# Batch 0 of a Nyström attention and MLP kernel: two blocks of the second layer beside the first layer's chunks, and a bank for the heads' products

## The chip, the core and the metric

The kernel runs on one core of one Trainium2 chip. The metric is the device time of one execution in microseconds, lower is better. Before the change the median of three runs is 324.2 us (323.54 to 325.01). Five engines work side by side, each in its own program order: TensorE (PE) multiplies, VectorE (DVE) and ScalarE (ACT) do elementwise work and here alone read PSUM, GpSimd (POOL) does elementwise work between SBUF tiles, SyncE (SP) issues DMAs.

## What is computed

For 8 batches with 8 heads of 576 x 64: landmarks are means over 18 rows of q and k (32 each), three softmax matrices are formed, one is inverted by six iterations, and the product gives 576 x 512 rows per batch. A two-layer MLP with a layer norm and a residual follows.

```python
A, Bm, C = sm(q, k_lm), sm(q_lm, k_lm), sm(q_lm, k)
Z = Bm.T / (norm1(Bm) * norminf(Bm) + 1e-6)
for _ in range(6):
    Z = 2 * Z - Z @ Bm @ Z
x = merge_heads(A @ Z @ C @ v)
out = x + relu(layer_norm(x) * g_ln @ w_ch1) @ w_ch2
```

## The kernel before

**The MLP works from the attention's factors.** The first layer's input rows are A times a small matrix per head, so w1 is multiplied by the heads' small matrices first (`product_of_heads`, tile psm, evicted to m), and a chunk m of 128 hidden units is m times ea, the softmax A, with the heads' four products in one 128-row contraction: four matmuls of 288 columns into psh, evicted with a relu into hT (`first_layer`, L758). There are 16 chunks (MCH) per batch, four for each of the four psm. The mean of the layer norm is taken out of w1 once (`less_mean`, psf, L747; `center_w1`, L753) and its scale is applied at the end. The second layer (`second_layer`, L798) takes blocks of 128 rows: 16 matmuls hT times w2 into one PSUM bank (pso), then one DVE instruction that scales and adds the residual rows x (xblk), then a store from SP. There are 36 blocks over all batches, 4 for an even batch and 5 for an odd one; in an even batch the last 64 rows of hT are copied by POOL to the front of the next batch's hT (L802). In batch 0 alone a block is done in two halves of 256 columns, since w2 is loaded and cast in pieces of half the columns (`load_w2`, L210; `cast_w2`, L216).

**Attention.** `attention0` (L282) handles batch 0, `attention2` (L608) the others in sets of batches: (1), (2), (3, 4), (5, 6), (7). In order: psb (landmark scores), psec (scores of k, evicted by ACT's exp to ec and turned by DVE to ecT), psse (norms), pscv (C times v), six times psn with a DVE update st (`iterate`, L425), meanwhile psea (scores of q, exp to ea), and `normalize` (L270), which sums heads by PE (psd), takes Ln and Exp on ACT (lns) and multiplies ea by DVE (batches 0 and 1) or POOL; then pszt and pszc, copied to zt and zcbd. From zt on the first layer of that batch can begin (`ready`). `rows_of` (L439) makes the rows x for the residual and the statistics (psy, xblk, six).

**Preparation.** `Coming` (L459) brings a set: loads (SP), casts to nat (POOL), turns to xT (DVE), and sums over the segments to part, by DVE (`add_up`, two reductions) or by POOL (four additions to asum and s, then a small DVE turn sT), then `spread` (PE psl, ACT lm). `sums_by_dve` says for how many units q is summed by DVE; k always is.

**PSUM.** The pools hold eight banks: ps1 one, ps2 two buffers of two banks (tag p2: pst, psc, psa, psd, psec, psea, psm, psh, pscv, pszt, pszc), psM three buffers of one bank (tag pm: idle, psf, psl, psy, pso, psg and batch 0's small tiles). A buffer is given to the next tile when the last one has been read.

**Order.** Every engine instruction that is wrapped by `keep` stands in the order of the program text, engine by engine. The MLP is a generator, `mlp` (L828), that is advanced by `fill(n)` (L852) by n times 512 columns of PE work wherever the attention leaves room; `mlp` puts one step of the next batch's first layer behind each 2048 columns of the second layer, once that batch is ready, and does the rest alone afterwards. The lists `steps` (L943) say, for each step of an attention, how many columns to fill and how many casts and jobs of the next set to do. Batch 0's prologue is written out by hand (L883 to L939): six iterations with `scale_w1`, `less_mean`, `center_w1` and `warm` matmuls between them, and then fills, jobs of set 1 and rows of batch 0. Helpers record most instructions, so the profile has L75 for matmuls and L69 for DVE, ACT and POOL; the tiles tell them apart.

Of the kernel before, what the change touches and what calls it, by code (L numbers as in the profile page):

```python
# [16 lines left out]
P = 128  # L17
# [3 lines left out]
def kernel(  # L21
# [188 lines left out]
    def load_w2(i):  # L210
        part, m = divmod(i, 4)
        stg = stage.tile([P, 4, DM // 2], FP32, name="wstg", tag="stg")
        keep(nc.sync.dma_start(out=stg[:], in_=w2_src[:, ts(m, 4), ts(part, DM // 2)]))
        w2_coming.append(stg)

    def cast_w2(i):  # L216
        part, m = divmod(i, 4)
        pool.tensor_copy(out=w2_16[:, ts(m, 4), ts(part, DM // 2)], in_=w2_coming[i][:])
# [12 lines left out]
    psM = ctx.enter_context(tc.tile_pool(name="psM", bufs=3, space=bass.MemoryType.PSUM))  # L231

    def warm(n, cols):
        idle = psM.tile([P, 512], FP32, name="idle", tag="pm")
        for _ in range(n):
            MM(idle[:, 0:cols], zeros[:, 0:P], zeros[:, 0:cols])
# [33 lines left out]
    def normalize(ea, engine):  # L270
        pss = ps2.tile([P, 2, 512], FP32, name="psd", tag="p2")
        for half in range(2):
# [4 lines left out]
        engine.tensor_tensor(out=ea, in0=ea, in1=lns[:].rearrange("p a t -> p (a t)"),  # L277
                             op=ALU.mult)
# [3 lines left out]
    def attention0():  # L282
# [58 lines left out]
        def scores_of_q(w):  # L341
            psa = p2([P, NJ, 64], FP32, "psa")
            for (j0, j1) in ((0, 8), (8, NJ)):
                for h in range(4):
# [8 lines left out]
        extra = [lambda: scores_of_q(0), lambda: scores_of_q(1), lambda: product(0),  # L353
                 lambda: product(1), lambda: normalize(ea[0], dve), lambda: normalize(ea[1], dve)]
# [3 lines left out]
        rcv = asm.tile([P, W], FP32, name="rcv", tag="rcv")  # L358
        for it in range(6):
            st = iterate(p1, st, it, W)  # L360
            if it == 4:
# [5 lines left out]
            extra[it]()  # L367
# [16 lines left out]
        ready.add(0)  # L384
        yield "zt"
        for w in range(W):
            dve.tensor_tensor(
                out=zcbd_buf[w][:], in0=pszc[:, w, None, :].broadcast_to([P, 4, D]),
                in1=mask4[:, :, None].broadcast_to([P, 4, D]), op=ALU.mult)
# [49 lines left out]
    def rows_of(bs, ea, zcbd):  # L439
        for i, b in enumerate(bs):  # L440
            t0 = 0
            while t0 < S:
# [4 lines left out]
                psy = psM.tile([P, 512], FP32, name="psy", tag="pm")  # L447
# [11 lines left out]
    class Coming:  # L459
        def __init__(self, bs, sums_by_dve=0):  # L460
            self.bs, self.sums_by_dve = bs, sums_by_dve
# [7 lines left out]
            for i, (nm, w) in enumerate(self.parts[:2 * n]):  # L469
                self.jobs.append((self.turn, i))  # L470
                if nm == "k" or w < sums_by_dve:
                    self.jobs.append((self.add_up, i))
# [25 lines left out]
        def cast(self, i):  # L498
# [11 lines left out]
            if nm == "q" and w >= self.sums_by_dve:  # L510
# [40 lines left out]
        def spread(self, y):  # L551
            part = self.part.pop(y)
            psl = psM.tile([P, 2, 8, LM], FP32, name="psl", tag="pm")
# [54 lines left out]
    def attention2(bs, c):  # L608
# [8 lines left out]
        for y in range(W // 2):  # L617
# [11 lines left out]
            yield  # L629
# [35 lines left out]
        if not late:  # L665
            for y in range(W // 2):
                product(y)
                if y + 1 < W // 2:
                    yield
            product_done()  # L670
        yield

        for it in range(6):
# [9 lines left out]
            yield  # L683
# [10 lines left out]
        for i, b in enumerate(bs):  # L694
            heads[b] = (ea[U * i:U * i + U], zt, U * i)
            ready.add(b)
# [13 lines left out]
        yield  # L710

        yield from rows_of(bs, ea, zcbd_buf[z0:z0 + W])
# [34 lines left out]
    def less_mean(f):  # L747
        psf = psM.tile([P, 512], FP32, name="psf", tag="pm")
        for c in range(KCH):
            MM(psf[:], lesser[:], w1_16[:, c, ts(f, 512)], start=(c == 0), stop=(c == KCH - 1))  # L750
        scalar.copy(less(f), psf[:])

    def center_w1(f, c, n):  # L753
# [4 lines left out]
    def first_layer(b):  # L758
        room_for(b)
        hT, base = hTs[b], 64 * (b % 2)  # L760
        ea, zt, w0 = heads.pop(b)
        m16 = {}

        def product_of_heads(f):
            psm = ps2.tile([P, 2, 512], FP32, name="psm", tag="p2")
            for r in range(2):
                for e in range(2):
                    for u in range(U):
                        block = 2 * r + e if b == 0 else 2 * (e ^ u) + r
                        rows = ds(64 * e, 64)  # L770
                        MM(psm[ds(32 * block, 32), u, :], zt[rows, r, w0 + u, :],
                           w1_16[rows, 2 * u + r, ts(f, 512)], rb=64 * e, cb=32 * block)
            m16[f] = t = mprod.tile([P, U, 512], FP16, name="m16", tag="m16")
            if f % 2 == 0:
                scalar.copy(t[:], psm[:])
            else:
                dve.tensor_copy(out=t[:], in_=psm[:])

        product_of_heads(0)
        yield 512  # L780
        for m in range(MCH):
            f = m // 4
            if b == 0 and m in (1, 4):
                less_mean(2 if m == 1 else 3)
                yield 2048
                center_w1(2 if m == 1 else 3, 0, 4)
            if m % 4 == 1 and f < 3:
                product_of_heads(f + 1)
                yield 512
            psh = ps2.tile([P, 2, 512], FP32, name="psh", tag="p2")  # L790
            for half in range(2):
                for u in range(U):
                    MM(psh[:, half, 0:HS], m16[f][:, u, ts(m % 4, P)], ea[u][:, ts(half, HS)],
                       start=(u == 0), stop=(u == U - 1))
            act(hT[:, m, ds(base, S)].rearrange("p (a t) -> p a t", a=2), psh[:, :, 0:HS], AF.Relu)
            yield 4 * HS

    def second_layer(b):  # L798
        hT = hTs.pop(b)
        if b % 2 == 0:  # L800
            room_for(b + 1)
            pool.tensor_copy(out=hTs[b + 1][:, :, 0:64], in_=hT[:, :, S - 64:S])  # L802
        blocks = range(4 + b % 2)
        order = [(u, None) for u in blocks] if b else [(u, p) for p in (0, 1) for u in blocks]
        for u, p in order:
# [182 lines left out]
```

## Time and profile before

| what | value |
|---|---|
| median of 3 runs | 324.2 us |
| profiled execution, its own time | 323.97 us |
| its span | 321.9 us |
| granted PE clock, mean | 0.968 |
| first chunk of batch 0 (psh) starts | 27.9 us |
| psb of batch 1 starts | 49.2 us |
| first pso starts | 52.2 us |
| psl of batch 2 starts | 83.6 us |
| last chunk's eviction starts | 300.9 us |
| eviction of psh with relu (ACT), mean | 651 ns x128 |
| eviction of psm, ACT and DVE, mean | 1012 and 1207 ns, x16 each |

A line of the timeline gives start, length, engine, source line, operation, output tile<-input tiles, shape and count; in brackets the idle time before it and what ended it. A wait is put down to what came last. PE's busy time is modelled for pipelined matmuls, so the count of columns says more about PE than its busy share.

### The profile page before, as it was taken

To read this page: it belongs to the slowest core of one execution; us is meant where nothing else is said; L and a number is where in the kernel's file an instruction comes from. 1 tells how busy PE (TensorE), PEld (TensorE's weight loads), DVE (VectorE), ACT (ScalarE), POOL (GpSimd) and SP (SyncE) were. 2 spreads that over 40 slices of the span, in tenths; PEclk is the share of its full clock that TensorE was granted. 3 is DMA by queue.
4 is the path that set the end of the run, shared out by engine and by line. 5 is a ranking of instruction groups with operands and counts; after the bars stand their busy time and mean duration, and the time that the engine had idled before them with its cause. 6 is when DMAs were issued, how large, how long until landed. Compare 5 with 4: busy or idle time off the path is not lost.

```text
span 321.9 us, 8232 instructions
## 1 busy us (share of the span) xinstructions
PE 281.5 (87%) x3475; PEld 156.5 (49%) x3475; DVE 172.9 (54%) x369; ACT 175.8 (55%) x289; POOL 127.2 (40%) x154
## 2 busy tenths in 40 slices
PE   7767767989679688999898899999997999999995
PEld 7532434747353344454544444555553455455544
DVE  2555983549776695337995874446450345312112
ACT  2474764437453385595557557675756455454300
POOL 4389975921408996654956413310001100100000
PEclk9996996999799799999999999999999999999999
DMA  7999996164856962850795072111111112121133
GB/s 259 393 386 363 319 264 243 35 179 112 266 164 225 244 210 66 314 170 17 201 279 169 9 186 54 38 35 33 38 40 25 35 35 66 33 59 41 35 82 81
DMA packets 26173, 46.67 MB, mean 145 GB/s; under 512 B 2452, under 2 KB 7832, under 8 KB 26136
## 3 DMA queue, kind: packets, MB, share of 16 engines
q1 hardware_dynamic: 25976, 46.02, 47.6%
q8 instruction: 27, 0.44, 0.6%
q10 hardware_dynamic: 160, 0.13, 0.2%
q14 instruction: 10, 0.08, 0.1%
HBM read 36.70 MB, written 9.44 MB: 143 GB/s over the span
## 4 chain that ended last, share of the span: by engine, by line
PE 58%; DVE 18%; ACT 15%; issue 4%; POOL 2%; DMA 2%; SPq 1%; ACTq 0%; POOLq 0%; DVEq 0%
PE pso L75 29%; PE psh L75 14%; ACT hT L69 5%; DVE six L69 4%; DVE part L69 4%; DVE xT L69 3%; ACT m L69 3%; PE psm L75 3%; DMA stg<-in_k_dram 2%; DVE w L69 2%; PE pscv L75 2%; ACT lns L69 2%; ACT ec L69 2%; PE psec L75 1%; PE psn L75 1%
## 5 line engine op out<-in xcount | busy, mean ns | idle before, releaser
L75 PE MATMUL pso<-w,hT 128*128 128x512 f16 (+1 forms) x656 | 156.0, 360 | 0.0
L69 ACT ACTIVATE hT<-psh 128x576 f16<-128x576 f32 x128 | 81.8, 651 | 56.1 <-PE psh L75 55.4
L75 PE MATMUL psh<-ea,m 128*128 128x288 f16 x512 | 84.5, 290 | 13.8 <-ACT hT L69 5.6
L75 PEld LDWEIGHTS <-hT 128*128 128x128 f16 x656 | 61.3, 100 | 45.8 <-issue 10.2
L75 PEld LDWEIGHTS <-m 128*128 128x128 f16 x512 | 49.9, 99 | 48.2 <-issue 17.8
L69 DVE SCALAR_TENSOR_TENSOR xblk<-pso,rstd,xblk 128x512 f32<-128x512 f32 (+1 forms) x41 | 27.8, 678 | 40.0 <-PE pso L75 39.7
L69 POOL CAST nat<-stg 128x1152 f16<-128x1152 f32 x28 | 32.3, 1169 | 22.5 <-DMA stg<-in_k_dram 9.5
L69 POOL TENSOR_TENSOR ea<-ea,lns 128x576 f16<-128x576 f16 x12 | 15.4, 1284 | 56.7 <-ACT lns L69 56.7
L69 DVE BATCH_NORM_STATS2 six<-xblk 128x6 f32<-128x512 f32 x36 | 24.7, 685 | 20.0 <-ACT xblk L69 19.8
L69 POOL CAST natv<-stg 128x1152 f16<-128x1152 f32 x16 | 18.3, 1164 | 30.2 <-DMA stg<-in_v_dram 27.9
L69 DVE SCALAR_TENSOR_TENSOR st<-st,psn 128x128 f16<-128x128 f16 (+2 forms) x36 | 11.3, 315 | 32.2 <-PE psn L75 32.2
L69 ACT CAST m<-psm 128x1024 f16<-128x1024 f32 x16 | 16.2, 1012 | 20.0 <-PE psm L75 20.0
L69 ACT COPY xblk<-psy 128x512 f32<-128x512 f32 (+1 forms) x40 | 23.4, 588 | 5.2 <-PE psy L75 4.9
L69 DVE CAST m<-psm 128x1024 f16<-128x1024 f32 x16 | 19.3, 1207 | 11.7 <-PE psm L75 11.7
L69 DVE TENSOR_REDUCE part<-xT 128x32 f16<-128x576 f16 x32 | 22.4, 741 | 0.1
L69 DVE STREAM_TRANSPOSE xT<-nat 128x576 uint32<-128x576 uint32 x28 | 21.3, 761 | 1.6 <-POOL nat L69 1.6
L75 PE MATMUL psm<-w,zt 64*32 64x512 f16 x256 | 14.6, 400 | 5.6 <-DVE zt L69 3.8
L69 POOL COPY hT<-hT 128x1024 f16<-128x1024 f16 x4 | 4.1, 1037 | 34.2 <-ACT hT L69 34.2
L75 PE MATMUL psy<-zcbd,ea 128*128 128x256 f16 (+1 forms) x80 | 15.5, 278 | 0.0
L69 POOL TENSOR_TENSOR asum<-nat 128x512 f32<-128x512 f16 x12 | 15.1, 1258 | 1.0
L69 POOL TENSOR_TENSOR asum<-asum 128x256 f32<-128x256 f32 (+1 forms) x24 | 14.2, 592 | 1.9
L69 ACT ACTIVATE ec<-psec 128x576 f16<-128x576 f32 x14 | 10.3, 807 | 3.9 <-PE psec L75 3.9
(108 smaller groups left out, 251.7 us busy)
## 6 DMA issues: line engine op xcount, KB each, us to landing
stg<-in_q_dram SPq DMA_DIRECT2D x16, 576.0 KB, 5.8
stg<-in_k_dram SPq DMA_DIRECT2D x16, 576.0 KB, 6.8
wstg<-in_moe_w_ch_dram SPq DMA_DIRECT2D x16, 512.0 KB, 6.7
out_dram<-xblk SPq DMA_DIRECT2D x62, 128.0 KB, 2.3
stg<-in_v_dram SPq DMA_DIRECT2D x9, 576.0 KB, 6.9
stg<-in_v_dram SPq DMA_DIRECT2D x14, 288.0 KB, 5.1
out_dram<-xblk SPq DMA_DIRECT2D x18, 64.0 KB, 2.0
out_dram<-xblk ACTq DMA_DIRECT2D x2, 64.0 KB, 2.2
```

The costliest lines, as they stand in the source:

```text
L69: return lambda *args, **kw: keep(getattr(self.engine, op)(*args, **kw))
L75: keep(nc.tensor.matmul(o, l, r, start=start, stop=stop, tile_position=(rb, cb), skip_group_check=(skip or cb != 0)))
```

## The change

The second layer's blocks 0 and 1 of batch 0 now accumulate in psM's two buffers while the first layer's chunks are made (`blocks_0_and_1`), behind chunks 9 to 15; `second_layer(0)` keeps blocks 2 and 3, of full width. w2 is loaded and cast in pieces of two whole rows of 128. A new pool psA of one bank takes idle, psf, psm, psl, psy and psg; psm is made for one unit u at a time, half as wide, u 0 evicted by ACT and u 1 by DVE. The prologue is re-ordered: psd in iterations 2 and 3, ea of unit 0 scaled by halves in 3 and 4, that of unit 1 after zt, `less_mean(0)` split, the centering of f 0 after zt, fewer warm calls. DVE evicts chunks 5, 8, 11 and 14 of batch 0, and each third chunk where a first layer runs alone. Attention of batch 1 begins behind chunk 14. A step of the first layer says itself how many columns of the second layer have to follow (`gap`), and none is done while an attention step is `quiet`. `Coming` is given the list of parts that DVE sums. In the code left out psl, psy and psg move to psA, `Coming` looks parts up in that list, and the yields of `attention2` after its scores give True, all others False.

```diff
@@ -208,14 +208,12 @@
-    part, m = divmod(i, 4)
-    stg = stage.tile([P, 4, DM // 2], FP32, name="wstg", tag="stg")
-    keep(nc.sync.dma_start(out=stg[:], in_=w2_src[:, ts(m, 4), ts(part, DM // 2)]))
+    stg = stage.tile([P, 2, DM], FP32, name="wstg", tag="stg")
+    keep(nc.sync.dma_start(out=stg[:], in_=w2_src[:, ts(i, 2), :]))
...
-    part, m = divmod(i, 4)
-    pool.tensor_copy(out=w2_16[:, ts(m, 4), ts(part, DM // 2)], in_=w2_coming[i][:])
+    pool.tensor_copy(out=w2_16[:, ts(i, 2), :], in_=w2_coming[i][:])
@@ -228,10 +226,11 @@
-psM = ctx.enter_context(tc.tile_pool(name="psM", bufs=3, space=bass.MemoryType.PSUM))
+psM = ctx.enter_context(tc.tile_pool(name="psM", bufs=2, space=bass.MemoryType.PSUM))
+psA = ctx.enter_context(tc.tile_pool(name="psA", bufs=1, space=bass.MemoryType.PSUM))
...
-    idle = psM.tile([P, 512], FP32, name="idle", tag="pm")
+    idle = psA.tile([P, 512], FP32, name="idle", tag="pa")
@@ -267,15 +266,17 @@
-def normalize(ea, engine):
+def divisors(ea):
...
-    engine.tensor_tensor(out=ea, in0=ea, in1=lns[:].rearrange("p a t -> p (a t)"),
-                         op=ALU.mult)
+    return lns[:].rearrange("p a t -> p (a t)")
...
+def normalize(ea, engine):
+    engine.tensor_tensor(out=ea, in0=ea, in1=divisors(ea), op=ALU.mult)
@@ -350,21 +351,32 @@
-    extra = [lambda: scores_of_q(0), lambda: scores_of_q(1), lambda: product(0),
-             lambda: product(1), lambda: normalize(ea[0], dve), lambda: normalize(ea[1], dve)]
...
+    lns = []
...
+    def scale_ea(w, half):
+        cols = ts(half, HS)
+        dve.tensor_tensor(out=ea[w][:, cols], in0=ea[w][:, cols], in1=lns[w][:, cols],
+                          op=ALU.mult)
...
     for it in range(6):
         st = iterate(p1, st, it, W)
+        if it < 2:
+            scores_of_q(it)
+        if it in (2, 3):
+            product(it - 2)
+            lns.append(divisors(ea[it - 2]))
...
-        extra[it]()
+        if it in (3, 4):
+            scale_ea(0, it - 3)
         yield "iteration"
@@ -381,8 +393,10 @@
-    ready.add(0)
...
+    scale_ea(1, 0)
+    scale_ea(1, 1)
+    yield "softmax"
@@ -666,9 +680,9 @@
-                yield
+                yield False
...
-    yield
+    yield False
@@ -680,7 +694,7 @@
-        yield
+        yield it < W // 2
@@ -707,9 +720,10 @@
-    yield
...
-    yield from rows_of(bs, ea, zcbd_buf[z0:z0 + W])
+    yield False
+    ready.update(bs)
+    for _ in rows_of(bs, ea, zcbd_buf[z0:z0 + W]):
+        yield False
@@ -744,68 +758,97 @@
-def center_w1(f, c, n):
+psf_of = {}
...
+def less_mean(f, c0=0, c1=KCH):
+    if c0 == 0:
+        psf_of[f] = psA.tile([P, 512], FP32, name="psf", tag="pa")
+    for c in range(c0, c1):
+        MM(psf_of[f][:], lesser[:], w1_16[:, c, ts(f, 512)], start=(c == 0),
+           stop=(c == KCH - 1))
+    if c1 == KCH:
+        scalar.copy(less(f), psf_of.pop(f)[:])
...
+def center_w1(f, c=0, n=KCH):
...
+class First:
+    def __init__(self, b):
+        room_for(b)
+        self.b, self.hT = b, hTs[b]
+        self.ea, self.zt, self.w0 = heads.pop(b)
+        self.m16 = {}
...
+    def product_of_heads(self, f, u):
+        b, zt = self.b, self.zt
+        if u == 0:
+            self.m16[f] = mprod.tile([P, U, 512], FP16, name="m16", tag="m16")
+        psm = psA.tile([P, 512], FP32, name="psm", tag="pa")
         for r in range(2):
             for e in range(2):
...
+                block = 2 * r + e if b == 0 else 2 * (e ^ u) + r
+                rows = ds(64 * e, 64)
+                MM(psm[ds(32 * block, 32), :], zt[rows, r, self.w0 + u, :],
+                   w1_16[rows, 2 * u + r, ts(f, 512)], rb=64 * e, cb=32 * block)
+        t = self.m16[f][:, u, :]
+        if u == 0:
+            scalar.copy(t, psm[:])
         else:
...
+            dve.tensor_copy(out=t, in_=psm[:])
...
+    def chunk(self, m, by_dve=False):
         psh = ps2.tile([P, 2, 512], FP32, name="psh", tag="p2")
         for half in range(2):
             for u in range(U):
...
+                MM(psh[:, half, 0:HS], self.m16[m // 4][:, u, ts(m % 4, P)],
+                   self.ea[u][:, ts(half, HS)], start=(u == 0), stop=(u == U - 1))
+        o = self.hT[:, m, ds(64 * (self.b % 2), S)].rearrange("p (a t) -> p a t", a=2)
+        if by_dve:
+            dve.tensor_scalar(out=o, in0=psh[:, :, 0:HS], scalar1=0.0, scalar2=None,
+                              op0=ALU.max)
+        else:
+            act(o, psh[:, :, 0:HS], AF.Relu)
...
+alone = [False]
...
+def first_layer(b):
+    l1 = First(b)
+    for u in range(U):
+        l1.product_of_heads(0, u)
+        yield 512, 1024
+    for m in range(MCH):
+        f = m // 4
+        if f < 3 and m % 4 in (1, 2):
+            l1.product_of_heads(f + 1, m % 4 - 1)
+            yield 512, 512
+        l1.chunk(m, alone[0] and m % 3 == 2)
+        yield 4 * HS, 2048
...
+def keep_tail(b):
     if b % 2 == 0:
         room_for(b + 1)
...
+        pool.tensor_copy(out=hTs[b + 1][:, :, 0:64], in_=hTs[b][:, :, S - 64:S])
...
+def finish_block(b, u, pso, part=None):
+    j = 9 * (b // 2) + 4 * (b % 2) + u
+    last = j == NBLK - 1
+    cols = ts(part or 0, DM if part is None else DM // 2)
+    x = x_blk[j]
+    dve.scalar_tensor_tensor(out=x[:, cols], in0=pso[:],
+                             scalar=rstds[b][:, u:u + 1], in1=x[:, cols],
+                             op0=ALU.mult, op1=ALU.add)
+    store(j, x, cols, last)
+    if part != 0:
+        x_blk.pop(j)
...
+def second_layer(b):
+    hT = hTs[b]
+    blocks = range(4 + b % 2) if b else (2, 3)
+    for u in blocks:
+        last = b == B - 1 and u == 4
+        for part in ((0, 1) if last else (None,)):
             n = DM if part is None else DM // 2
             cols = ts(part or 0, n)
             pso = psM.tile([P, n], FP32, name="pso", tag="pm")
@@ -816,27 +859,26 @@
+            if u == blocks[-1]:
+                hTs.pop(b, None)
+            finish_block(b, u, pso, part)
...
+quiet = [False]
...
-    yield from first_layer(0)
     for b in range(B):
-        ahead, done, owed = None, False, 0
+        ahead, done, owed, gap = None, False, 0, 0
+        if b:
+            keep_tail(b)
         for cols in second_layer(b):
             yield cols
             if ahead is None and b + 1 in ready:
                 ahead = first_layer(b + 1)
             owed += cols
-            if ahead and not done and owed >= 2048:
-                owed -= 2048
-                cols = next(ahead, None)
+            if ahead and not done and owed >= gap and not quiet[0]:
+                owed = min(owed - gap, 4096)
+                cols, gap = next(ahead, (None, 0))
@@ -844,7 +886,10 @@
             while b + 1 not in ready:
                 yield 0
-            yield from ahead or first_layer(b + 1)
+            alone[0] = True
+            for cols, _ in ahead or first_layer(b + 1):
+                yield cols
+            alone[0] = False
@@ -859,11 +904,13 @@
-sets = [Coming((1,), 1), Coming((2,)), Coming((3, 4), 1), Coming((5, 6)), Coming((7,))]
+sets = [Coming((1,), ("k0", "k1", "q0", "q1")), Coming((2,), ("k0", "k1")),
+        Coming((3, 4), ("k0", "k1", "k2", "q0")), Coming((5, 6), ("k0", "k1")),
+        Coming((7,), ("k0",))]
@@ -910,37 +957,68 @@
     next(a0)
     if it == 0:
         scale_w1(1, 1, scalar)
-    if it < 3:
+    if it < 2:
...
     if it == 3:
-        less_mean(0)
+        less_mean(0, 0, 2)
+    if it == 4:
+        less_mean(0, 2, 4)
...
-    if it == 4:
-        center_w1(0, 0, 2)
-        warm(1, 384)
-    if it == 5:
-        center_w1(0, 2, 2)
-        scale_w1(5, 1, scalar)
-        warm(1, 384)
...
-fill(1)
+center_w1(0)
+next(a0)
...
-center_w1(1, 0, 4)
-scale_w1(7, 1, scalar)
-next(a0)
-for count in (6, 4, 6, 4, 4, 4, 4):
-    fill(count)
-    b1.next_job()
-for _ in range(5):
-    fill(2)
-    next(a0, None)
-while b1.jobs:
-    b1.next_job()
-    fill(2)
...
+l1 = First(0)
+l1.product_of_heads(0, 0)
+l1.product_of_heads(0, 1)
+center_w1(1)
+scale_w1(5, 1, scalar)
+accs = []
...
+def blocks_0_and_1(m):
+    for u in range(2):
+        if m == 0:
+            accs.append(psM.tile([P, DM], FP32, name="pso", tag="pm"))
+        MM(accs[u][:], hTs[0][:, m, ts(u, P)], w2_16[:, m, :],
+           start=(m == 0), stop=(m == MCH - 1))
...
+a1 = attention2((1,), b1)
+for m in range(MCH):
+    l1.chunk(m, m in (5, 8, 11, 14))
+    if m == 0:
+        next(a0)
+        scale_w1(7, 1, scalar)
+    if m in (2, 3):
+        l1.product_of_heads(1, m - 2)
+    if m == 2:
+        less_mean(2)
+        center_w1(2)
+    if m == 4:
+        less_mean(3)
+    if m in (5, 6):
+        l1.product_of_heads(2, m - 5)
+    if m == 6:
+        center_w1(3)
+    if m in (9, 10):
+        l1.product_of_heads(3, m - 9)
+    if m in (4, 7, 8, 11, 12):
+        next(a0)
+    if m >= 3:
+        b1.next_job()
+    if m >= 9:
+        blocks_0_and_1(2 * (m - 9))
+        blocks_0_and_1(2 * (m - 9) + 1)
+    if m == 14:
+        assert not b1.jobs
+        next(a1)
+keep_tail(0)
+blocks_0_and_1(14)
+blocks_0_and_1(15)
+for u in range(2):
+    finish_block(0, u, accs[u])
...
-steps = [[(5, 0, 0)] * 2 + [(5, 0, 0)] * 6 + [(6, 1, 0)] + [(6, 1, 1)] * 5]
+steps = [[(4, 0, 0)] + 6 * [(3, 0, 0)] + [(4, 1, 0)] + 5 * [(6, 1, 1)]]
@@ -949,7 +1027,8 @@
-    for (count, casts, jobs), _ in zip(plan, attention2(c.bs, c)):
+    attention = a1 if c is b1 else attention2(c.bs, c)
+    for (count, casts, jobs), quiet[0] in zip(plan, attention):
```

## The prediction

> **What bounds the kernel now.** I read the page's busy table and chain first, then engine busy time by stage, then the timeline of single engines.
>
> ```profile
> PE 281.5 (87%) x3475; PEld 156.5 (49%) x3475; DVE 172.9 (54%) x369; ACT 175.8 (55%) x289; POOL 127.2 (40%) x154
> ...
> PE 58%; DVE 18%; ACT 15%; issue 4%; POOL 2%; DMA 2%; SPq 1%; ACTq 0%; POOLq 0%; DVEq 0%
> ```
>
> TensorE (PE) leads, but an average mixes stages. By stage (columns: stretch, length, then busy us and instruction count per engine, granted PE clock, DMA share, GB/s):
>
> ```profile
> 25.00:30.50 5.50, 5.29 (x24) 1.93 (x28) 1.85 (x4) 2.78 (x5) 5.21 (x6) 0.55 1.05 368
> 30.50:46.30 15.80, 12.40 (x96) 7.00 (x88) 15.63 (x24) 11.44 (x19) 14.61 (x15) 1.00 0.98 301
> 46.30:49.20 2.90, 0.03 (x1) 0.00 (x0) 0.78 (x3) 2.02 (x6) 1.49 (x2) 1.00 1.04 300
> 49.20:56.00 6.80, 5.82 (x100) 3.58 (x109) 2.43 (x9) 2.75 (x5) 3.21 (x4) 0.59 0.64 235
> ...
> 67.00:83.60 16.60, 12.10 (x112) 7.77 (x112) 12.98 (x29) 10.36 (x18) 2.39 (x3) 1.00 0.66 198
> 83.60:106.00 22.40, 18.93 (x307) 10.37 (x307) 15.06 (x36) 10.26 (x17) 11.64 (x12) 0.92 0.63 200
> 106.00:121.00 15.00, 12.47 (x87) 6.62 (x88) 11.52 (x25) 10.15 (x18) 14.01 (x17) 0.89 0.83 231
> 121.00:300.90 179.90, 168.95 (x2113) 89.48 (x2112) 90.75 (x189) 109.41 (x180) 51.28 (x54) 1.00 0.32 88
> 300.90:321.90 21.00, 17.27 (x96) 9.18 (x94) 3.97 (x6) 0.65 (x1) 0.00 (x0) 1.00 0.27 63
> ```
>
> From 30.5 to 46.3, batch 0's first layer, VectorE (DVE) is busy 15.63 of 15.8 us: DVE bounds it, and PE has room. Then PE stands still for 2.9 us and comes back at a clock of 0.59. From 121 on PE is 94% busy and bounds the rest; the last 17 us are pure second layer. So PE work that is pulled into the first 56 us is worth its full time later, if nothing between 56 and 121 becomes later.
>
> ```profile
> 49.22 0.27 PE L75 MATMUL psb<-lm 32*32 32x32 f16 x16 [2.89 <-ACT lm L69]
> 53.56 2.31 PE L75 MATMUL pso<-w,hT 128*128 128x256 f16 x10
> 58.50 1.25 PE L75 MATMUL pso<-w,hT 128*128 128x256 f16 x10
> 83.61 0.39 PE L75 MATMUL psl<-part,spread 128*128 128x256 f16 x2 [2.96 <-DVE part L69]
> ```
>
> The same ten half-width pso matmuls take 2.31 us after the stall and 1.25 us five us later. From the tail, 96 matmuls (64 of 512, 32 of 256 columns) in 17.3 us: 0.216 us per 512 columns; a chunk of psh (4 x 288) is then 0.49 us.
>
> **Skill, weighed against the change.** PE waited 2.9 us and the 10 matmuls after it ran at about half rate. The Trainium skill, "TensorE: Matmul & The Clock Gate" (Part 1), puts the return to half clock at an idle window of about 3.4 us; here gaps of 2.89 and 2.96 us were enough. By either, the change's removal of three warm calls (iterations 2, 4 and 5) before 25 us can cost clock; but the clock is already 0.55 at 25 to 30.5, so the sum takes nothing for it.
>
> **Part by part** (one execution of 323.97 us, span 321.9 and 2.07 around it; the median of the runs is 324.2, 0.2 above).
>
> 1. *Prologue.* Before zt (24.88) DVE does two ea multiplications of 1.03 and two centerings of 0.68 that wait for ACT's lns (to 21.6). Now psd is issued in iterations 2 and 3, the multiplications are halved, and those of unit 1 and the whole centering come after zt. Ln and Exp of unit 0 follow ea (17.9) at 0.65 + 0.68: 19.2; scale half 0.55, st, cv 0.7, half 0.55, last st: 21.4; zt about 22. Centering 1.23 to 1.9, two halves 1.1, then less_mean(1), psm, its two evictions through one bank (about 0.6 each): chunk 0 at 26.0 instead of 27.88. **-1.9 us.**
>
> 2. *DVE in batch 0's first layer.* A DVE read of 576 PSUM columns is not in the trace; between CAST 128x128 (0.28) and 128x1024 (1.21) a line gives 0.75, and 0.68 for 512; the ends are 0.5 and 1.2. To the last add-up DVE now has: centerings 1.23 + 1.9 + 1.85, zcbd 0.75, three psm halves 2.0, four turns 3.1, four add-ups 5.6 (q1's is new at 1.4; its sT and part, 0.49, go), three block statistics 2.6, two relus 1.5: 20.5 us, from 26.0 to 46.5, against 43.8 before, where the statistics came later. Then PE has chunks 12 to 14, a psy and four times four pso before the attention scores: 3 x 0.49 + 0.2 + 16 x 0.216 = 5.1. psb at about 51.6 instead of 49.22: **+2.4 on the attention chain**, with the 1.9 inside it. But PE does not stand still: nearly all 32 pso of blocks 0 and 1 (6.9 us) lie in this stretch, under DVE's work.
>
> 3. *w2.* Blocks 0 and 1 need all columns of rows m, hence loads of two whole rows. POOL loses q1's sum here, 3.9 us, and w2's casts follow at 32.2 if the loads are there:
>
> ```profile
> 32.22 2.00 POOL L69 TENSOR_TENSOR asum<-nat 128x512 f32<-128x512 f16 x1
> 34.30 1.27 POOL L69 TENSOR_TENSOR asum<-asum 128x256 f32<-128x256 f32 x2
> 35.65 0.43 POOL L69 TENSOR_TENSOR s<-asum,nat 128x128 f16<-128x128 f32 x1
> 36.02 8.92 POOL L69 CAST w<-wstg 128x1024 f16<-128x1024 f32 x8
> ```
>
> Eight loads of 0.52 MB at the 340 to 388 GB/s of 14 to 40 us take 11 to 12.3 us, so they end by 43 at the latest, when m = 9 begins. Cost 0; if that is late, PE waits some 2 us.
>
> 4. *Attention of batch 1.* Before: 49.22 to zt at 66.81, 17.6 us, with 1 chunk and 77 half matmuls (8.4 us). Now PE's clock holds: of 6.8 us at 0.59, 2.2 saved; and the fill is 8 + 26 matmuls (7.3 us): 1.1 less. 51.6 + 14.3 = 65.9: **-0.9**. Of batch 0's second layer 51 halves (5.5 us) were still owed here; now 6 matmuls (1.3): **-4.2**. Set 2's loads now stand behind the stores of blocks 0 and 1 in SP's queue, about 52 instead of 43.98; POOL's casts were held by the hT copy until 54.13 anyway, and its sums (to 65.7) had 7 us before the first turn at 72.9: 0, or +2 if the DMA is slow.
>
> 5. *Batch 1's first layer.* alone[0] gives DVE each third relu: some four, +3.0, against 0.8 less for whole evictions. DVE had 3.6 us free in 67 to 83.6, so I take half, **+1.1** at psl (83.61); PE does four more chunks meanwhile, **-2.0**.
>
> 6. *quiet and gap.* In attention 2, iterations lie 1.6 to 2.0 us apart, but psn at 91.27 and 95.33 lie 4.06 apart, with psea and psh fighting over two ps2 buffers. quiet takes the chunks away: 2 us, half of it kept, as POOL's ea follows: **-1.0**.
>
> 7. *psm in one bank of its own.* From 121 PE waits 2.5 us for m in psh, 1.7 for ec in psm, 0.5 for m in psec. I take half: **-2.3**. The ends: -4.7, and +3 where psy, psm and psl, all in one bank, wait for an eviction of 0.6 each. The Trainium skill ("Trainium Kernel Development and Optimization", Best Practices) asks for double buffers, against this single one; were each of the 64 psm evictions exposed at 0.59 (row: less, 128x512), it would be +38. The matmuls put between them (a chunk 0.49, pso 0.43 and more) speak for the row.
>
> 8. *Sums.* k3, then k2 and k3, then k1 go from DVE to POOL: 4 x 2.85 = 11.4 us on POOL, DVE 4 x (1.4 - 0.49) less. POOL is busy 14.01 of 15 in 106 to 121, so one sum (k3) can show there whole; later POOL has 51 of 180. I take **+1.5**; ends 0 and +5.8 (two sums ahead of ea at 139).
>
> 9. *Not all keeps its worth:* PE waits for zt (104.2 to 106.25) and for part whatever was done ahead. **+1.2.**
>
> Sum: -0.9 - 4.2 + 1.1 - 2.0 - 1.0 - 2.3 + 1.5 + 1.2 = **-6.6**; 323.97 - 6.6 = **317.4 us**.
>
> **Rivals.**
> - *A: swallowed.* Attention 2 and its preparation, not PE, set the time until 121; what is ahead at 66 turns into longer PE waits. Terms 4's -4.2 and 5's -2.0 go, 7 stays small: about 323.0. For: 2.96 and 1.99 us waits there. Against: PE had 18.93 of 22.4.
> - *B: slower.* DVE is the new bound of the attention chain: it has 2.4 us more before psb and up to 3.0 in the relus before psl. If the clock does not hold (4's 2.2 is lost), psl(2) comes at 83.6 + 2.4 + 2.2 = 88 and POOL's sums add 2.85 behind it: the chain ends 6 to 7 late, PE's advance of 4.2 is used up: 326.5. It decides when psl of set 2 is over 4 us later than 83.6.
> - *C: more.* 7 gives its 4.7, 8 and 9 cost nothing, 1 helps: 311.
>
> **Chances.** Forecast (313 to 322.5) 0.53; C 0.14; A 0.14; B 0.19. Half a per cent, 1.6 us, is about what a measurement of this kernel can tell from no change; A lies across that bound. Faster 0.70, same 0.11, slower 0.19. The range takes in A, nearly all of B and the better part of C: 310 to 326.5.
>
> **What would show it.** Right: clock 1.00 from 30 to 56; 32 full-width pso before 52; psb near 51.6 and zt of batch 1 near 66; psn of attention 2 evenly spaced. Wrong: psb past 54, psl of set 2 past 87, waits of psm, psy or psl for ACT above 5 us, POOL full from 97 to 125 with PE waiting for part behind it.

## The result

The changed kernel takes 354.84 us (median of four runs, 350.68 to 355.58); the kernel before, run beside it, 323.87 us. The ratio is 1.0926, 95% interval 1.0835 to 1.1017: **31 us slower**, where 6.6 us faster was forecast. Medians are over all runs; ratios leave out a run in the slower state that executions on this chip sometimes show (one run each of e1, e12 and e13 below). The profiled execution of after took 355.1 us, span 353.4.

The page of after: the busy line, the granted clock in 40 slices, and two groups (busy us, mean ns of one | idle time before them and what ended most of it).

```profile
PE 300.5 (85%) x3408; PEld 154.0 (44%) x3408; DVE 182.1 (52%) x396; ACT 171.4 (48%) x291; POOL 132.3 (37%) x166
...
PEclk9985896999999769999999999999999999999999
...
L75 PE MATMUL psm<-w,zt 64*32 64x512 f16 x256 | 26.9, 409 | 13.8 <-ACT xblk L69 7.9
...
L75 PE MATMUL psy<-zcbd,ea 128*128 128x256 f16 (+1 forms) x80 | 16.4, 287 | 11.7 <-DVE m L69 6.3
```

and the same two groups in before:

```profile
L75 PE MATMUL psm<-w,zt 64*32 64x512 f16 x256 | 14.6, 400 | 5.6 <-DVE zt L69 3.8
...
L75 PE MATMUL psy<-zcbd,ea 128*128 128x256 f16 (+1 forms) x80 | 15.5, 278 | 0.0
```

TensorE is busy 19 us longer with fewer matmuls, and 12.3 of the 19 are in psm: the same 256 matmuls of nearly the same mean length were 14.6 us before. Idle time ahead of psm and psy has grown by 19.9 us; idle time elsewhere has shrunk, so that all of it together has grown by 12.5. What TensorE waited for in after (us in total, times, longest):

```profile
PE psm L75 <- ACT xblk L69: 7.9, 14, 0.8
PE psy L75 <- DVE m L69: 6.3, 7, 2.2
PE psm L75 <- ACT m L69: 4.3, 9, 1.1
...
PE psy L75 <- ACT m L69: 2.5, 4, 1.1
```

psm and psy wait for each other's evictions, and psm for its own (xblk is psy's eviction, m is psm's): the new single bank, and many small waits, none over 2.2 us. Stages of after (columns as in the stages of before); 52.6 is its psl of batch 1, 61.1 psb of batch 1, 94.0 psl of batch 2, 332.4 the last chunk's eviction:

```profile
33.00:46.00 13.00, 9.30 (x53) 4.11 (x52) 10.12 (x14) 6.20 (x12) 9.22 (x9) 0.80 0.92 307
46.00:52.60 6.60, 3.51 (x22) 1.58 (x20) 6.53 (x13) 1.79 (x3) 0.95 (x1) 0.94 0.00 0
52.60:61.10 8.50, 8.45 (x32) 3.70 (x32) 2.15 (x4) 2.77 (x6) 0.00 (x0) 0.65 0.01 3
...
94.00:133.70 39.70, 32.88 (x367) 15.35 (x368) 27.07 (x62) 16.62 (x30) 25.76 (x30) 0.87 0.62 188
133.70:332.40 198.70, 178.65 (x2118) 91.42 (x2118) 92.94 (x205) 110.94 (x189) 59.09 (x66) 1.00 0.28 77
332.40:353.40 21.00, 17.28 (x96) 9.19 (x94) 4.41 (x7) 0.65 (x1) 0.00 (x0) 0.97 0.32 75
```

The loss is spread out. Start of each, in us:

| | before | after | later by |
|---|---|---|---|
| zt of batch 0 | 24.9 | 22.2 | -2.7 |
| psb of batch 1 | 49.2 | 61.1 | 11.9 |
| zt of batch 1 | 66.8 | 75.7 | 8.9 |
| psl of batch 2 | 83.6 | 94.0 | 10.4 |
| zt of batches 3, 4 | 144.5 | 160.3 | 15.8 |
| zt of batches 5, 6 | 206.4 | 225.5 | 19.1 |
| last chunk's eviction | 300.9 | 332.4 | 31.5 |

Some 10 us are lost before 61 us; 21 us in the rest, where TensorE bounds. The tail (21.0 us) is the same. The timeline of TensorE in after shows both kinds of loss:

```profile
48.48 0.65 PE L75 MATMUL psh<-ea,m 128*128 128x288 f16 x4
51.33 0.38 PE L75 MATMUL psy<-zcbd,ea 128*128 128x256 f16 x2 [2.20 <-DVE m L69]
52.65 0.61 PE L75 MATMUL psl<-part,spread 128*128 128x256 f16 x2 [0.94 <-DVE part L69]
53.05 1.91 PE L75 MATMUL pso<-w,hT 128*128 128x512 f16 x4
...
77.78 0.40 PE L75 MATMUL psm<-w,zt 64*32 64x512 f16 x4 [0.67 <-ACT xblk L69]
...
78.86 0.40 PE L75 MATMUL psm<-w,zt 64*32 64x512 f16 x4 [0.36 <-ACT m L69]
```

After two waits of 2.20 and 0.94 us four pso take 1.91 us (the stage from 52.6 has a clock of 0.65); at 45.82 four took 1.04. And four psm matmuls take 0.40 us. In before, eight take no longer from batch 1 on; in its batch 0 they do (both stages at clock 1.00):

```profile
39.37 0.62 PE L75 MATMUL psm<-w,zt 64*32 64x512 f16 x8
...
69.41 0.41 PE L75 MATMUL psm<-w,zt 64*32 64x512 f16 x8
```

Each of these matmuls uses 64 rows and 32 columns of the array. `block` gives unit 0 and unit 1 of a batch above 0 complementary places, and there the eight of both units take 0.41 us; in batch 0 it gives both units the same four places, and eight take 0.62. So the eight of a later batch run beside each other, and with one unit at a time half of the array is empty for as long.

### The profile page after: what moved, and what is told of

Read it like the earlier page. It is cut to its first block, busy times and chain, and to the rows that moved or that the text cites. A ratio compares the mean times of both kernels' runs of the same rounds, so it can differ in the third digit from the quotient of the medians.

```text
span 353.4 us, 8129 instructions
## 1 busy us (share of the span) xinstructions
PE 300.5 (85%) x3408; PEld 154.0 (44%) x3408; DVE 182.1 (52%) x396; ACT 171.4 (48%) x291; POOL 132.3 (37%) x166
## 4 chain that ended last, share of the span: by engine, by line
PE 61%; DVE 16%; ACT 14%; issue 3%; DMA 3%; POOL 1%; SPq 1%; ACTq 0%; POOLq 0%; DVEq 0%
PE pso L75 30%; PE psh L75 15%; PE psm L75 5%; ACT hT L69 3%; ACT xblk L69 3%; DVE m L69 3%; DVE six L69 2%; ACT m L69 2%; DVE part L69 2%; PE psy L75 2%; ACT lns L69 2%; DMA stg<-in_k_dram 2%; PE psn L75 1%; DVE xT L69 1%; DVE w L69 1%
## 5 line engine op out<-in xcount | busy, mean ns | idle before, releaser
L69 ACT ACTIVATE hT<-psh 128x576 f16<-128x576 f32 x114 | 73.4, 648 | 68.4 <-PE psh L75 67.6
L75 PE MATMUL psh<-ea,m 128*128 128x288 f16 x512 | 89.2, 299 | 11.0 <-DVE m L69 3.4
L75 PEld LDWEIGHTS <-hT 128*128 128x128 f16 x592 | 56.1, 99 | 53.9 <-issue 16.0
L69 DVE BATCH_NORM_STATS2 six<-xblk 128x6 f32<-128x512 f32 x36 | 24.9, 691 | 33.3 <-ACT xblk L69 33.1
L75 PE MATMUL psm<-w,zt 64*32 64x512 f16 x256 | 26.9, 409 | 13.8 <-ACT xblk L69 7.9
L69 DVE CAST m<-psm 128x512 f16<-128x512 f32 x32 | 21.8, 682 | 23.6 <-PE psm L75 23.3
L69 ACT CAST m<-psm 128x512 f16<-128x512 f32 x32 | 18.7, 583 | 14.0 <-PE psm L75 14.0
L69 POOL CAST natv<-stg 128x1152 f16<-128x1152 f32 x16 | 18.2, 1163 | 17.2 <-DMA stg<-in_v_dram 9.7
L75 PEld LDWEIGHTS <-zt 64*32 64x32 f16 x256 | 8.6, 89 | 34.4 <-issue 33.1
L69 POOL TENSOR_TENSOR asum<-asum 128x256 f32<-128x256 f32 (+1 forms) x30 | 17.7, 590 | 2.4
L69 DVE TENSOR_REDUCE part<-xT 128x32 f16<-128x576 f16 x26 | 18.1, 736 | 0.0
L69 POOL TENSOR_TENSOR asum<-nat 128x512 f32<-128x512 f16 x15 | 17.3, 1155 | 1.2
```

The source lines that it names most:

```text
L69: return lambda *args, **kw: keep(getattr(self.engine, op)(*args, **kw))
L75: keep(nc.tensor.matmul(o, l, r, start=start, stop=stop, tile_position=(rb, cb), skip_group_check=(skip or cb != 0)))
```

## The experiments

Two theories: *the bank and the units* (term 7: products one unit at a time, in one bank) and *batch 0* (everything before 61 us comes late, and the rest follows). Each kernel was timed beside the kernel before on the same chip; ratios are to that, with their 95% interval.

**1. Products of heads whole again, in two banks of ps2; psy alone in ps2 instead; the one bank alone on before; bank and units on before.**

```diff
 e1: after
-psm = psA.tile([P, 512], FP32, name="psm", tag="pa")
+psm = ps2.tile([P, 2, 512], FP32, name="psm", tag="p2")   (8 matmuls, one eviction)
 e2: after
-psy = psA.tile([P, 512], FP32, name="psy", tag="pa")
+psy = ps2.tile([P, 512], FP32, name="psy", tag="p2")
 e3: before; idle, psf, psl, psy, psg to psA (1 bank), psM 2 buffers
 e4: e3 with product_of_heads(f, u): 4 matmuls, one eviction of 128x512 each, in psA
```

> The changed kernel with psm again made for both units at once (8 matmuls, two banks of ps2, one eviction); all else of the change stays. Theory 'bank': the loss comes from psm by units in the one bank of psA, 12.3 us more busy time of psm on PE (26.9 against 14.6) and some 22 us of PE waits for evictions of that bank: 322 to 332 us. Rival 'batch 0': the loss comes from the late attention of batch 1 (zt at 75.7 against 66.8) and from set 2's loads behind the stores (68.4 against 42.5 us), psm costs little: 345 us or more.

> The changed kernel with only psy moved from psA to ps2, so that psm and psy no longer take turns in one bank; psm stays by units. Theory 'bank': the waits psm for xblk (7.9), psy for m (8.8) and some of the rest go, the 12 us of psm's halves stay: 334 to 342 us. Rival 'batch 0': 350 us or more.

> The kernel before with only the pools changed: psM two buffers, psA one bank for idle, psf, psl, psy and psg; psm stays whole in ps2. Both theories: the small tiles alone are rarely waited for, 323 to 329 us; if it is over 335, psy and psl in one bank are a cost by themselves that neither theory has.

> The kernel before with the pools of the change and psm by units in psA, unit 1 behind the next chunk; batch 0, the sums, the pace and the loads are as before. Theory 'bank': most of the loss shows here without the rest of the change: 348 to 360 us. Rival 'batch 0': 325 to 335 us.

Measured: e1 342.56 (1.0513, 1.0464 to 1.0563); e2 341.72 (1.0541, 1.0476 to 1.0607); e3 326.6 (1.0028, 1.0005 to 1.005); e4 348.22 (1.0709, 1.0666 to 1.0753). The bank for the small tiles costs under 2 us. With the products by units in it the cost is 22.8 us on before. e2, which takes psy alone out of the bank, gains 13 to 15 of the 31, and its idle time is 1.5 us ahead of psy and 8.5 ahead of psm: psm and psy in turns are the costly pair. But e1, which undoes units and their bank together, gains only 13 or 14 of the 31: neither theory alone explains after.

**2. The pace.** e5 gives e1 the old pace (one piece of the first layer per 2048 columns); e6 adds the loads of set 2 ahead of the stores; e7 gives before the new pace; e8 gives after the old one.

```diff
 e5, e8
-if ahead and not done and owed >= gap and not quiet[0]:
-    owed = min(owed - gap, 4096)
+if ahead and not done and owed >= 2048:
+    owed -= 2048
 e6: as e5, and ahead of attention2((1,), b1)
+for _ in range(4):
+    sets[1].next_load()
```

> The changed kernel with psm whole (as in e1) and with the old pace: one step of the next first layer behind each 2048 columns of the second layer, no quiet steps. Theory 'pace': what is left of the loss in e1 (342.6 against 325.4) comes from chunks that no longer have pso between them (12 psh in a row at 142 us in e1, each pair waiting for its eviction) and the half clock behind it: 326 to 333 us. Rival 'late set 2': it comes from batch 0's late attention and set 2's late loads: 338 to 343 us.

> e5 and set 2's four loads issued before batch 0's chunks, ahead of the stores of blocks 0 and 1 in SP's queue. Theory 'pace': POOL has slack there, within 2 us of e5. Rival 'late set 2': 5 us or more below e5, as set 2's casts come back from 67 to about 55 us.

> The kernel before with the change's pace alone: gap by piece, at most 4096 owed, no step of the first layer while an attention step is quiet; psm, banks, batch 0, sums and loads as before. Theory 'pace': slower by itself, 332 to 342 us. Rival 'late set 2': 322 to 328 us, as the pace only matters with late sets.

> The changed kernel with the old pace alone put back (psm by units in psA stays). Theory 'pace' and 'bank' as separate costs: 354.8 less what e5 gains on e1, about 340 to 346 us. If psm's bank is the only thing that matters once it is there, 350 or more.

Measured: e5 331.48 (1.0228, 1.0158 to 1.0299); e6 333.4 (1.0271, 1.023 to 1.0312); e7 331.94 (1.0239, 1.0197 to 1.0281); e8 353.82 (1.0926, 1.085 to 1.1002). Each against its own before, the new pace costs 7.6 us on before and 9 to 10 on e1, but nothing clear of noise in after: the prices do not simply add. The early loads bring nothing, though they are issued at 40.7 us instead of 60.5: psl of batch 2 comes at 87.5 (86.7 in e5) and is not bound by them. What the pace does is seen at batches 3 and 4. TensorE in e1:

```profile
124.31 1.25 PE L75 MATMUL pso<-w,hT 128*128 128x512 f16 x5
...
126.50 1.25 PE L75 MATMUL pso<-w,hT 128*128 128x512 f16 x5
...
135.80 0.21 PE L75 MATMUL psn<-st 32*32 32x64 f16 x4 [2.27 <-issue]
...
142.19 2.62 PE L75 MATMUL psh<-ea,m 128*128 128x288 f16 x12 [0.80 <-ACT ea L69]
...
145.65 1.52 PE L75 MATMUL psh<-ea,m 128*128 128x288 f16 x8
```

and in before:

```profile
137.40 1.03 PE L75 MATMUL pso<-w,hT 128*128 128x512 f16 x4
138.26 0.65 PE L75 MATMUL psh<-ea,m 128*128 128x288 f16 x4
...
139.32 1.03 PE L75 MATMUL pso<-w,hT 128*128 128x512 f16 x4
140.19 0.65 PE L75 MATMUL psh<-ea,m 128*128 128x288 f16 x4
```

Before puts one chunk behind four pso, and ACT has that time to evict it. In the quiet steps pso runs by itself; later the chunks come three in a row, with only two ps2 buffers and an eviction of 0.65 us for each, and partly at half clock (0.50 from 144 to 146). Between 121 and 146 us TensorE is busy 22.01 us at clock 1.00 in e5, which differs from e1 in the pace alone, and 19.13 at 0.87 in e1. That this bunching is what costs is argued, not shown. e7, the pace alone on before, has the same fives of pso at 124.03 and 126.24 but at most two chunks in a row, clock 1.00 and 21.61 us busy (before 23.00); its idle time ahead of psh, 18.2 us against 13.8, is 4.4 of its 7.6. And e9 of part 4, with the old pace, is busy only 19.63 us in that window.

**3. Is it the units or the bank; quiet or gap?** e14 puts the units in ps2 buffers, without the bank; e16 has the gaps but no quiet steps, both on before.

```diff
 e14: before with product_of_heads(f, u)
+psm = ps2.tile([P, 512], FP32, name="psm", tag="p2")
 e16: as e7
-if ahead and not done and owed >= gap and not quiet[0]:
+if ahead and not done and owed >= gap:
```

> The kernel before, with the products of heads one unit at a time (as e4, +23), but each in a buffer of the ps2 pool that chunks use, with no bank of its own that psy, psl and psf share. If e4's 23 us are lost packing and more steps in the queue: 338 to 347. If they are the waits for the one bank: 326 to 332. By the rows of the changed kernel packing is 12 us of busy time and the waits 25, of which some overlap: I expect 334 to 338.

> The kernel before, with the new pace's gaps between pieces (1024, 512, 2048, the debt kept up to 4096) but without its quiet steps. Gaps and quiet steps together were +7.6. If the quiet steps are the cost, because the second layer is used up in them with no chunk beside it: 323 to 326. If the gaps themselves thin the chunks out: 330 to 332.

Measured: e14 335.54 (1.0345, 1.0303 to 1.0388), +10.7 on the before of its chip; e16 328.69 (1.012, 1.0069 to 1.0171), +3.9. The groups of e14:

```profile
L75 PE MATMUL psm<-w,zt 64*32 64x512 f16 x256 | 24.7, 397 | 9.1 <-DVE zt L69 3.9 <-ACT ec L69 1.7 <-DVE w L69 1.0
...
L75 PE MATMUL psy<-zcbd,ea 128*128 128x256 f16 (+1 forms) x80 | 15.5, 278 | 0.0
```

and of e4:

```profile
L75 PE MATMUL psm<-w,zt 64*32 64x512 f16 x256 | 26.5, 402 | 16.5 <-ACT m L69 6.8 <-ACT xblk L69 4.3 <-DVE zt L69 3.9
...
L75 PE MATMUL psy<-zcbd,ea 128*128 128x256 f16 (+1 forms) x80 | 15.8, 279 | 8.4 <-ACT m L69 3.6 <-DVE m L69 2.4 <-ACT xblk L69 1.2
```

Without the bank psm is still busy 10.1 us longer than before (24.7 against 14.6), psy waits for nothing, and the kernel is 10.7 us longer: about what the lost places beside each other take. It is not an exact match: the profiled execution is the slowest of e14's six (338.16 us), it has 3.5 us more idle time ahead of psm, and twice as many evictions come with the units, which no run separates (idle time ahead of psh is that of before, 13.9 against 13.8). The bank brings the other 12.1 us of e4 (22.8 less 10.7), with 7.4 more idle time ahead of psm and 8.4 ahead of psy, but 8.4 less ahead of psh (5.5 against 13.9): psm no longer takes ps2's buffers there. The quiet steps are the other 3.7 us of e7; what the gaps do for their 3.9 was not taken apart.

**4. What e5 has left.** e9 is e5 with the old division of the sums; e10 is e9 without the relus on DVE; e12 is e9 with the small tiles back among three psM buffers; e11 and e15 are before with the new sums alone and with the DVE relus alone; e13 is e9 with both undone, so batch 0's part alone.

```diff
 e9                                      (e11: the reverse, for k, on before)
-Coming((3, 4), ("k0", "k1", "k2", "q0")), Coming((5, 6), ("k0", "k1")),
+Coming((3, 4), ("k0", "k1", "k2", "k3", "q0")), Coming((5, 6), ("k0", "k1", "k2", "k3")),
...                                      (q1 of set 1 back to POOL, k1 of set 7 back to DVE)
 e10, e13                                (e15: the reverse, on before)
-l1.chunk(m, alone[0] and m % 3 == 2)
+l1.chunk(m)
...                                      (chunks 5, 8, 11 and 14 of batch 0 likewise)
 e12, e13
-psA.tile(..., tag="pa")
+psM.tile(..., tag="pm")                 (psM with 3 buffers)
```

> The changed kernel with the heads' products whole, the old pace and the old division of the landmark sums (the k sums of the third to seventh batch back on VectorE). Without the last of the three it was 331.5, 7 above before. If the sums moved to GpSimd hold up batches 5 and 6 (there the second set of landmark products came 5 us late, behind a GpSimd that waited 4.45 us for a free buffer): 325 to 328, with psl of batches 5 and 6 near 169.5 and 174. If the 7 us come from the shared bank or from batch 0: 330 to 332.

> As e9, and every relu of the first layer on ScalarE again, as before. If the relus on VectorE delay the landmarks and softmaxes that VectorE does for the next batch: 1 to 2 us less than e9. If they relieve ScalarE, which then ends the waits for psh and for the one bank: 1 to 3 us more than e9. In batch 0 (four chunks) and in the stretches where the first layer runs alone, the sign may differ; zt(1) and zt(7) tell which.

> The kernel before, with one part of the change alone: four k sums (of batches 4, 6 and 7) go from VectorE to GpSimd. If the sums cost what e5 had left: 327 to 330, psl of batches 5 and 6 some 4 us late. If GpSimd's sums only hurt together with the shared bank: 323.5 to 325. My forecast had +1.5 for this (0 to +5.8), so 325.4.

> As e9, and the small tiles back among three banks with pso, as before: of the change there are left the re-ordered prologue, the second layer's weights by rows, batch 0's two blocks beside the first layer's chunks, and the relus on VectorE. If the one bank still costs where psl waits for ScalarE's copy out of it: 2 to 4 us less than e9, some 322 to 324, at or below before. If batch 0's reordering itself is a loss: as e9, 326 to 328.

> Of the change there are left only the re-ordered prologue, the second layer's weights by rows and batch 0's two blocks beside the first layer's chunks: products of heads whole, old pace, old sums, relus all on ScalarE, small tiles among three banks. The relus gave 3.4 us and the banks 2.4 when each was undone on e9 (330.85). If the two add: 325, 0 to 1 above before, and batch 0's reordering is worth nothing. If this part alone is a gain that the others hid: 320 to 323. If it is a loss: 327 and more.

> The kernel before, with the relus on VectorE alone (batch 0's chunks 5, 8, 11, 14, and every third chunk where the first layer runs by itself). If they cost by themselves what their removal gave on e9: 326 to 328. If only where batch 0's reordering loads VectorE: 324 to 325. My forecast had +1.1.

Measured: e9 330.85 (1.0196, 1.0172 to 1.0221); e10 327.44 (1.0094, 1.0073 to 1.0115); e11 325.92 (1.0033, 1.0003 to 1.0063); e12 328.46 (1.0102, 1.0067 to 1.0137); e13 327.66 (1.0105, 1.0068 to 1.0143); e15 328.39 (1.0114, 1.0067 to 1.0161). So the sums, which I took for e5's remainder, are not it: their return gave under 1 in e9, and alone they cost 1.5. The relus on DVE cost 3.4 in e9 and 3.6 alone. They stand ahead of the landmark sums in DVE's queue, as e15's DVE shows in batch 0's first layer:

```profile
39.15 1.40 DVE L69 TENSOR_REDUCE part<-xT 128x32 f16<-128x576 f16 x2
40.47 0.74 DVE L69 TENSOR_SCALAR hT<-psh 128x576 f16<-128x576 f32 x1
41.13 0.76 DVE L69 STREAM_TRANSPOSE xT<-nat 128x576 uint32<-128x576 uint32 x1
41.93 1.41 DVE L69 TENSOR_REDUCE part<-xT 128x32 f16<-128x576 f16 x2
43.26 0.75 DVE L69 TENSOR_SCALAR hT<-psh 128x576 f16<-128x576 f32 x1
```

DVE runs without a gap there, so two relus of 0.75 put part off by 1.5 us; chunks behind them wait too (PE 2.8 us for hT from DVE in all), and psl of batch 1, which stands behind those chunks, starts at 49.5 us instead of 45.3. By zt of batch 1 e15 is 3.6 us late (70.4 against 66.8). The banks gave 2.4 (e9 to e12), but no more on top of e10: e13 is not below it. Batch 0's part alone is 2.8 us slower.

**5. Batch 0 alone: where?** e17 has the re-ordered prologue alone on before; e18 is e13 with the landmark product of batch 1 (spread, psl) queued behind chunk 13 instead of chunk 10.

```diff
 e18
-if m >= 3:
+if 3 <= m <= 9 or m == 13:
     b1.next_job()
```

> The kernel before, with the re-ordered prologue alone (scores of q, products and divisors two steps earlier, fewer idle multiplications, ScalarE's scalings of the first weights moved). In every kernel that has it, zt of batch 0 comes 2.1 to 3.1 us earlier. If that head start lasts: 321.5 to 323, below before. If the stages behind it wait for VectorE's landmark work or for GpSimd's casts of the weights, which it doesn't move: 324 to 326, with psb of batch 1 at 48.5 to 50 as before.

> As e13 (batch 0's part alone, 327.66), with the landmark product of batch 1 queued behind chunk 13 in place of chunk 10. In e13 it held TensorE 4.7 us for VectorE's last sum, with chunks 11 to 15 and their pso behind it, and the clock fell to half after it. If this wait is batch 0's loss: psl at 44 to 46 with no wait, psb of batch 1 at 49 to 51, and 323 to 325, at or below before. If the loss lies later, in the loads of batch 2 behind the stores or in fewer pieces of second layer to fill with: 327 to 328.

Measured: e17 324.28 (0.9999, 0.9968 to 1.003); e18 324.1 (0.9971, 0.9943 to 1.0). e13's TensorE:

```profile
44.20 0.59 PE L75 MATMUL psl<-part,spread 128*128 128x256 f16 x2 [4.74 <-DVE part L69]
44.58 1.91 PE L75 MATMUL pso<-w,hT 128*128 128x512 f16 x4
```

e18's:

```profile
47.62 0.38 PE L75 MATMUL psl<-part,spread 128*128 128x256 f16 x2 [1.05 <-ACT xblk L69]
47.83 1.02 PE L75 MATMUL pso<-w,hT 128*128 128x512 f16 x4
```

In e13 psl held TensorE for 4.74 us, with chunks and pso behind it that were ready, and then the clock was half: the same four pso 1.91 us. In e18 they run meanwhile at full clock; psl is later, but psb of batch 1 starts at 50.1 us instead of 53.9, and batch 0's loss is gone. e18 has the lowest ratio of all runs, but its interval reaches 1.0: a gain over before is not shown. In e17 zt of batch 0 comes at 22.0 instead of 24.9, and 1.7 us of it are still there at zt of batch 2 (104.25 against 105.95). Then they are given back: the second psl of batches 3 and 4 starts at 120.3 (120.8 in before), and what POOL waited for between 100 and 125 us in e17 begins with

```profile
POOL nat L69 <- DMA stg<-in_k_dram: 1.9, 1, 1.9
```

which before does not have there. That load is issued at 115.96 us (116.35 in before), behind two stores in SP's queue: most of the head start is gone there.

## Why the prediction was wrong, point by point

The step that failed is **term 7**, -2.3 with ends -4.7 and +3: alone on before it measured **+22.8** (e4, 348.22 against 325.43). I counted evictions and took the halves of psm as two cheap pieces with work between them; the sum put the psm matmuls' own time at nothing. Two things were missed. First, a matmul group's length does not halve with its number when its members run beside each other: 0.40 us for four in after, 0.41 for eight in before. The page of before let one suspect it (256 matmuls of 400 ns mean, but 14.6 us busy, 57 ns each). That is 10.7 us in e14. Second, the +3 for the single bank priced waits where a few would be exposed; psm and psy alternate in it through the rest of the kernel, and each stands in TensorE's queue ahead of what follows. That is 12.1 us, the bank of e3 (some 1 us) with it. The Trainium skill, "Trainium Kernel Development and Optimization" (Best Practices), asks to double-buffer, and names the overlap of DMA with compute; here it is a PSUM bank between TensorE and its evictions. The +38 worked out from a row beside it was too much; but the bank's single buffer did cost these 12.1 us, where I had sided with the matmuls in between as cover.

- *Term 1* (-1.9): right at its place, zt at 22.2 for about 22 and the first chunk's eviction 1.7 us earlier; worth nothing at the end (e17). The sum kept it inside the chain.
- *Term 2* (psb at 51.6): 61.1. DVE's last add-up ended at 52.6, not 46.5. DVE was not full: it stood 4.01 us before its centering at 33.2, where psf stood behind eleven psh at half clock and behind psm in the one bank (in e13, without that bank and at full clock, 2.08 and 0.41 us, and 30.6; how much of it is the bank's is not shown), and 2.64 us for xblk at 39.2. The 5.1 us of TensorE work between psl and psb became 8.5, since the clock was 0.65 after the waits, and psl stood in the queue at a place where it blocked ready work (e13, e18).
- *Term 3* (0): w2's casts held nothing up for more than 0.3 us (e13). Right.
- *Term 4* (-0.9 and -4.2): zt of batch 1 at 75.7 instead of 65.9. The clock did not hold. Set 2's loads were issued at 68.4, not 52; on e5, issuing them 20 us earlier gained nothing (e6). In e18, with clock 1.00 there, zt of batch 1 comes at 64.7, psl of batch 2 at 83.3 (83.6 in before), and the time is still that of before: the advance is swallowed there, as rival A had it (its 323.0 was a slip: its own terms give 323.6 with term 7 whole, and more with it small).
- *Term 5* (+1.1 and -2.0): the relus on DVE cost 3.6 alone (e15). Their price was right, their place wrong: the first four stand on DVE's full stretch ahead of psl, which term 2 counted and set against a gain of TensorE that did not come.
- *Term 6* (-1.0): +7.6 (e7), 3.7 of it for quiet steps and 3.9 for gaps. I looked at batch 2's attention alone, where the chunks disturb; what it costs over the rest is in part 2, and its cause is open.
- *Term 8* (+1.5): e11 measures +1.5 by medians (0.1 to 2.0 by the interval). Right.
- *Term 9* (+1.2): no run takes it apart; e17 shows one such loss, a head start of 2.9 us at zt of batch 0 that is gone by the end.
- *Rival B* decides as it said (psl of batch 2 over 4 us late: 94.0), but with 2.5 us it named under a tenth of the loss. Three of the signs of being wrong came: psb past 54, psl of set 2 past 87, and psm waiting 7.9 us for ACT's xblk.

The parts, each alone on before or by its removal: units 10.7, their bank 12.1, relus 3.6, batch 0 2.8, sums 1.5: 30.7 together, beside 31 measured. The near match is no proof that the parts add: the pace, 7.6 alone, adds nothing clear of noise in after (e8), and units and bank, 22.8 on before, give back only 13 or 14 when e1 undoes them. Why the pace hides behind the units was not tried.

## What to carry to other kernels

Ahead of splitting a group of small matmuls, divide its busy time by its count and compare that with the mean of one: where 57 ns stand against 400, suspect that the group lives from running side by side, and read from the code which places its members take; if the halves fall on complementary places, each takes as long as the whole. (Pipelining alone also parts the two figures, pso has 238 against 360 ns.) A PSUM bank that two steady producers share turns many evictions into waits of TensorE's queue, however short: the four rows of after are 34 waits, 21.0 us. A bank for tiles that come rarely was nearly free here (e3). And a product that waits for another engine belongs behind the work that is ready: moving one psl by three chunks was worth 3 to 4 us (e13, e18).

## What the runs showed of the hardware

- **Side by side.** Eight matmuls of 64 x 32 of the array, 512 columns, at complementary places: 0.41 us; eight at four places, each used twice: 0.62; four: 0.40.
- **The clock gate.** TensorE came back at half rate after waits of 2.20 and 0.94 us with one psy between them (after) and of 4.74 (e13): four pso 1.91 us. After waits of 1.47 and 1.05 us (e18) they took 1.02. The Trainium skill, "TensorE: Matmul & The Clock Gate" (Part 1), gives an idle window of about 3.4 us; the 4.74 agrees; the two short waits with a psy between them do not by themselves, and neither does the 2.27 of e1, with half rate behind it (three pso 1.46 us). Nor is the length of a wait alone what decides: after 3.12 us in e6 (psl at 47.1) four pso took 1.03 us.
